# A gated linear-attention and two-layer MLP kernel: norm work spread between recurrence steps, wider VectorE operations, and weight decoding moved between VectorE and ScalarE

## The chip, the cores and the metric

The kernel runs on one core of a Trainium2 chip. A core has the engines PE (TensorE, matrix products), DVE (VectorE), ACT (ScalarE), POOL (GpSimd, which here only issues transfers) and SP (SyncE, transfers too). The metric is device time in microseconds of one launch; less is better. The kernel before took 1100.47 us, the median of three runs (1099.94 to 1103.4).

## The reference

The inputs are float32. First comes a complex, gated linear attention over batch 4, 8 heads, 768 positions and head size 48, then two MLP blocks over the 3072 tokens of width 384:

```python
mag = sqrt(a_re**2 + a_im**2)
scale = minimum(mag, 0.999) / (mag + 1e-6)
ar, ai = a_re * scale, a_im * scale            # per position t and row d
for t in range(768):
    S_re, S_im = ar[t]*S_re - ai[t]*S_im + outer(k[t], v[t]), ar[t]*S_im + ai[t]*S_re
    y[t] = q[t] @ S_re
x = y as 3072 x 384
x = ((x @ w1) * (x @ w2) @ w3) @ w_out         # w1, w2: 384 x 1024; w3: 1024 x 1024; w_out: 1024 x 384
h = x @ w_in                                   # 384 x 2048
out = (h * tanh(softplus(h))) @ w_out2         # 2048 x 384
```

The kernel's weights arrive as 64-bit floats in two 32-bit words each, the low and the top word.

## The kernel before, in words

**Attention by chunks.** The tokens are cut into 24 chunks of 128, eight to a group, three groups. For every chunk the running products of the gates are needed from the chunk's middle to both sides. `bh_stream(g)` (L178 on) makes them for the eight chunks of group g at once: 128 partitions hold chunk halves and heads, and the 65 positions of a half go in ten blocks of seven (`BLK`; the last has two). For each block it loads the gates into `an` and k and q into `kqt`, by transfers that POOL issues. `norm(i)` (L203 to L243) turns block i's gates into scaled gates (`an`, with one part in both signs) and a factor `rv`: ACT squares, takes an inverse root and makes polynomials, DVE multiplies and limits. `steps(i)` (L245 on) then runs the recurrence: per position two DVE products and a sum for the running product `p` (L261, L263) and a product for `rv` (L262). After a block's seven steps it multiplies k and q by the running products into `kt` (L273, one instruction for each of two halves) and POOL stores `kt` to memory, `kq_d`. After the group's last block a small table `mt` follows.

**Chunks.** `ch_stream` loads a chunk's scaled k and q from `kq_d` (`tm`), transposes them on PE (L372), ACT copies them to `kf` and `qf` (L373), PE forms the scores, DVE masks them into `am` (L416), PE makes the output (`ps_y`), which goes through memory (`xd`) into tiles of 512 tokens.

**Weights.** `decode` (L135 to L156) rebuilds float32 values from the two words: ACT's Abs of the scaled top word gives the value without its low three mantissa bits and sign; a 16-bit ACT copy (L151) brings the low word's upper half beside the top word's, one DVE instruction shifts and masks (L152), and another shifts the value and joins the bits (L155). It is used on 11 pieces of 1024 elements per partition in `fold_stream`, which multiplies w3 by w_out once on PE (`ps_f`, L171), and on 48 pieces of 384 elements: 16 for w1 and w2 (`w12`), 16 for w_in (`win_stream`), 16 for the last weight in the first token tile of the last stage. `split` (L130, L131) cuts float32 into two parts of reduced precision, and `mm3` makes three PE products of them.

**MLPs.** `m1_stream` runs the first block per tile of 512 tokens (`pa`, `pb`, `acc`), the last stage the second (`ps_h`, sigmoid L637, Ln L644, tanh L649, `ps_o`).

**Order.** `_merge` draws from several streams by the costs that they yield: first the fold with group 0's `bh_stream`; then chunks 0 to 7, group 1 and part of the first MLP; then chunks 8 to 15, group 2 and more of it; then the last chunks and the MLP with w_in's decode; then the rest. That order gives priorities. A planner in the framework takes, for each engine, the ready instruction of highest priority by its own estimate of time, so each engine's queue can differ from the source: in the trace, instructions of `norm` stand between those of `steps`. Tiles with `bufs=1` have one buffer, and a new writer waits for the last reader.

Of the kernel before, what the change touches and what calls it, by code (L numbers as in the profile page):

```python
# [64 lines left out]
def kernel(  # L65
# [30 lines left out]
    msk = const.tile([CMAX, sum(SIZES)], F32, name="msk")  # L96
    sg = const.tile([128, 1], F32, name="sg")
    n_blk = [-(-(l + 1) // BLK) for l in GROUPS]
    flags = const.tile([128, sum(n_blk) + 1], F32, name="flags")
    wsum = const.tile([128, 64], F32, name="wsum")  # L100
    cb = const.tile([128, 3], F32, name="cb")
    fss = [const.tile([64, 2, D], F32, name=f"fs{z}") for z in range(2)]
# [31 lines left out]

    def decode(src, n, dst=None, raw=None, pool=None, cap=False):  # L135

        if raw is None:
            raw = (pool or stg).tile([128, n, 2], I32, tag="raw64", name="raw64")
        nc.sync.dma_start(out=raw.rearrange("p n z -> p (n z)"), in_=src.bitcast(I32))
        t = dst if dst is not None else stg.tile([128, n], I32, tag="dec", name="dec")  # L140
        f = t.bitcast(F32)
        i = n_flags[0]
        if not cap:
            n_flags[0] += 1
        top, r16 = raw[:, :, 1], raw.bitcast(U16)
        A.activation(
            out=f, in_=top.bitcast(F32), func=AF.Abs, scale=W_SCALE, accum_out=None if cap else wsum[:, i:i + 1]
        )
        if cap:
            V.tensor_scalar(out=f, in0=f, scalar1=W_MAX, scalar2=None, op0=ALU.min)  # L150
        A.copy(out=r16[:, :, 2], in_=r16[:, :, 1])  # L151
        V.tensor_scalar(  # L152
            out=top, in0=top, scalar1=13, scalar2=-0x7FFFFFF9, op0=ALU.arith_shift_right, op1=ALU.bitwise_and
        )
        V.scalar_tensor_tensor(out=t, in0=t, scalar=3, in1=top, op0=ALU.logical_shift_left, op1=ALU.bitwise_or)  # L155
        return f  # L156

    def fold_stream():
# [7 lines left out]
        for j in range(8):  # L166
            raw, dst = bufs[j % 3]
            f = decode(w3t[:, j], 1024, dst, raw).rearrange("p (k m) -> p k m", k=8)
            ps = mm_p.tile([128, HD], F32, tag="mm", name="ps_f")
            for kk in range(8):  # L170
                T.matmul(ps, lhsT=f[:, kk], rhs=wos[:, kk], start=(kk == 0), stop=(kk == 7))  # L171
            split(ps, woh[:, j], wol[:, j])
            for z, w in enumerate((woh, wol)):
                nc.sync.dma_start(out=w3o_d[:, z, j], in_=w[:, j].bitcast(F32))
            yield 2.0
# [5 lines left out]
    def bh_stream(g):  # L181
# [3 lines left out]
        blocks = [(s0, min(s0 + BLK, L + 1)) for s0 in range(0, L + 1, BLK)]  # L185
        ans, kqs, dec = {}, {}, {}
        run = {}
# [9 lines left out]
        def load_kq(i):  # L197
# [3 lines left out]
            nc.gpsimd.dma_start(out=kqs[i].rearrange("p s z d -> p s (z d)"), in_=kq[:, k0 + s0:k0 + s0 + m])  # L201

        def norm(i):  # L203
            s0, s1 = blocks[i]
            n = s1 - s0
            an = ans.pop(i)
            pad = [128, BLK, D]
            sq = bh.tile([128, n, 2, D], F32, tag="sq", name="sq", bufs=1, padded_shape=[128, BLK, 2, D])
            A.activation(out=sq, in_=an[:, :, 1:3], func=AF.Square)
            m2 = bh.tile([128, n, D], F32, tag="m2", name="m2", bufs=1, padded_shape=pad)  # L210
            V.tensor_tensor(out=m2, in0=sq[:, :, 0], in1=sq[:, :, 1], op=add)
            yield .5
            y0 = bh.tile([128, n, D], F32, tag="y0", name="y0", bufs=1, padded_shape=pad)
            A.activation(out=y0, in_=m2, func=AF.Abs_reciprocal_sqrt)
            fl, y2 = sq[:, :, 0], sq[:, :, 1]
            A.activation(out=y2, in_=y0, func=AF.Square)
            V.tensor_tensor(out=y2, in0=m2, in1=y2, op=mul)
            yield .5
            A.activation(out=fl, in_=y0, func=AF.Square, bias=cb[:, 0:1])
            A.activation(out=fl, in_=fl, func=AF.Relu, bias=cb[:, 1:2], accum_out=flags[:, f0 + i:f0 + i + 1])  # L220
            V.scalar_tensor_tensor(out=y0, in0=y2, scalar=-3.0, in1=y0, op0=add, op1=mul)
            yield .5

            p1, p2 = sq[:, :, 0], sq[:, :, 1]
            A.activation(out=p1, in_=y0, func=AF.Identity, scale=0.5e-6, bias=1.0)
            A.activation(out=p2, in_=y0, func=AF.Identity, scale=-0.5e-6, bias=1.0)
            rv = bh.tile([128, n, D], F32, tag="rv", name="rv", padded_shape=pad)
            V.scalar_tensor_tensor(out=p1, in0=y0, scalar=-2.0 / 0.999, in1=p1, op0=ALU.max, op1=mul)
            yield .5
            V.scalar_tensor_tensor(out=an[:, :, 2], in0=an[:, :, 2], scalar=sg[:, 0:1], in1=p1, op0=mul, op1=mul)  # L230
            yield .5
            A.activation(out=an[:, :, 0], in_=an[:, :, 2], func=AF.Copy, scale=-1.0)  # L232
            V.scalar_tensor_tensor(out=an[:, :, 1], in0=an[:, :, 1], scalar=-0.4995, in1=p1, op0=mul, op1=mul)
            yield .5
            V.scalar_tensor_tensor(out=p2, in0=y0, scalar=-2.0 / 0.999, in1=p2, op0=ALU.min, op1=mul)
            yield .5
            A.activation(out=rv, in_=p2, func=AF.Square, scale=0.5)
            if i == 0:
# [3 lines left out]
                V.memset(rv[0:64, 0], 1.0)  # L242
            dec[i] = (an, rv)  # L243

        def steps(i):  # L245
            s0, s1 = blocks[i]
            n = s1 - s0
            an, rv = dec.pop(i)
            p = bh.tile([128, n, 2, D], F32, tag="p", name="p", padded_shape=[128, BLK, 2, D])
            for j in range(n):  # L250
# [14 lines left out]
            run["p"], run["rv"] = p[:, n - 1], rv[:, n - 1]  # L265
            m = min(s1, L) - s0
            if m > 0:
                kqt = kqs.pop(i)
                V.tensor_tensor(out=kqt[:, :, 1], in0=kqt[:, :, 1], in1=rv[:, 0:m], op=mul)
                yield .5  # L270
                kt = bh.tile([128, m, 2, 2, D], F32, tag="kt", name="kt", bufs=1, padded_shape=[128, BLK, 2, 2, D])
                for z in range(2):
                    V.tensor_tensor(out=kt[:, :, z], in0=_bc(kqt[:, :, z], 2, 2), in1=p[:, 0:m], op=mul)  # L273
                    yield .8
                nc.gpsimd.dma_start(out=kq_d[g][0:64, s0:s0 + m], in_=kt[0:64].rearrange("p s z r d -> p s (z r d)"))
                for z in range(2):
                    nc.gpsimd.dma_start(
                        out=kq_d[g][64:128, s0:s0 + m, (1 - z) * D2:(2 - z) * D2],
                        in_=kt[64:128, :, z].rearrange("p s r d -> p s (r d)"),
                    )  # L280
            if s0 <= L - 1 < s1:
# [4 lines left out]
                if g == 0:  # L286
                    nc.gpsimd.dma_start(out=fss[0][0:8], in_=last[120:128])
            if i < len(blocks) - 1:
                return
            fs = fss[g % 2]  # L290
            x1 = bh.tile([64, 2, 2, D], F32, tag="x1", name="x1", bufs=1)
            mt = bh.tile([64, 4, D], F32, tag="mt", name="mt", bufs=1)
            bt = p[0:64, L - s0]
            V.tensor_tensor(out=x1[:, 0], in0=bt, in1=fs, op=mul)
# [5 lines left out]
            tabs[g] = mt  # L300
            yield 1.0

        load(0)
        load(1)
        load_kq(0)
        yield from norm(0)
        for i in range(len(blocks)):
            if i + 2 < len(blocks):
                load(i + 2)
            if i + 1 < len(blocks):  # L310
                if blocks[i + 1][0] < L:
                    load_kq(i + 1)
                yield from norm(i + 1)
            yield from steps(i)

# [6 lines left out]
    def ch_stream():  # L322
# [41 lines left out]
        def tr(n):  # L364
            C = chunks[n][2]
            kf[n] = ch.tile([D2, H, C], F32, tag="kf", name="kf", bufs=1)
            qf[n] = ch.tile([D2, H, C], F32, tag="qf", name="qf")
            for z, dst in ((0, kf[n]), (1, qf[n])):
# [572 lines left out]
```

## Time and profile before

| | before |
|---|---|
| median of the runs | 1100.47 us |
| profiled execution | 1102.09 us, span 1100.3 us |
| PE busy | 936.0 us, 85% |
| DVE busy | 686.9 us, 62% |
| ACT busy | 680.6 us, 62% |
| POOL busy | 109.3 us, 10% |
| mean granted clock of TensorE | 0.941 of full speed |

The span is the profiled part of the execution; about 1.8 us lie around it. Busy shares are means over stages that differ. The stages are: up to about 160 us the fold and group 0; from there to about 415 us groups 1 and 2 with chunks and the first MLP; to about 690 us the remaining chunks and the first MLP; then the second MLP.

### The profile page before, as it was taken

The numbers are of one execution on the slowest core, as the hardware profiler recorded it, in microseconds if no ns is written. First come the engines' busy times: TensorE is split into PE (matmuls) and PEld (weight loads), VectorE is DVE, ScalarE is ACT, GpSimd is POOL, SyncE is SP. The second block draws the span as 40 slices with busy tenths as digits, with TensorE's granted clock in tenths as the row PEclk, the third lists the DMA queues.
The fourth block names the chain that finished last, engine by engine and source line by source line (L and its number), as shares of the span: only waits on it lengthen the run. The fifth ranks groups of instructions, "written<-read, shape, count | busy, mean of one in ns | idle before, by whom it ended". The sixth has DMA issues, their size and how long they took to land.

```text
span 1100.3 us, 14021 instructions
## 1 busy us (share of the span) xinstructions
PE 936.0 (85%) x4952; PEld 756.6 (69%) x4952; DVE 686.9 (62%) x1513; ACT 680.6 (62%) x1203; POOL 109.3 (10%) x161
## 2 busy tenths in 40 slices
PE   0584008799799789999989999999999999999997
PEld 0342007687587678888878878877888888888876
DVE  4789998998899975263233532688465545555452
ACT  6884467777866753383543642898666745566672
POOL 1122342221223211000000000000000000000000
PEclk9896559799999979999989999999999999999999
DMA  7785579975845985342562420240100101000000
GB/s 275 231 251 143 130 187 276 240 207 152 221 135 151 232 198 140 90 149 65 148 143 47 123 86 1 89 123 19 34 24 1 58 1 58 1 10 20 1 29 32
DMA packets 72511, 124.37 MB, mean 113 GB/s; under 512 B 7575, under 2 KB 45777, under 8 KB 71025
## 3 DMA queue, kind: packets, MB, share of 16 engines
q1 hardware_dynamic: 60880, 85.41, 28.0%
q0 software_dynamic: 11552, 37.98, 12.5%
q8 instruction: 41, 0.67, 0.3%
q14 instruction: 38, 0.30, 0.1%
HBM read 84.16 MB, written 36.18 MB: 109 GB/s over the span
## 4 chain that ended last, share of the span: by engine, by line
PE 59%; ACT 15%; DVE 11%; DMA 10%; issue 5%; POOL 0%; SPq 0%; DVEq 0%; ACTq 0%; POOLq 0%
PE ps_o L500 16%; PE ps_h L500 13%; PE pa L500 6%; PE pb L500 6%; PE acc L500 5%; DMA xl<-xd 3%; PE ps_f L171 3%; PE ps_tr L372 2%; DMA xd<-ysb 2%; PE ps_a L415 2%; ACT raw L151 2%; DVE t L261 2%; PE ps_y L433 2%; DVE kt L273 1%; DMA an<-in_a 1%
## 5 line engine op out<-in xcount | busy, mean ns | idle before, releaser
L500 PE MATMUL ps_o<-gh,wuh 128*128 128x512 f32 x288 | 112.5, 396 | 6.0 <-ACT gh L130 4.6
L500 PE MATMUL ps_o<-gl,wuh 128*128 128x512 f32 x288 | 113.1, 393 | 0.4 <-DVE gl L131 0.4
L500 PE MATMUL ps_h<-x2h,wil 128*128 128x512 f32 x288 | 113.2, 393 | 0.0
L500 PE MATMUL ps_h<-x2h,wih 128*128 128x512 f32 x288 | 113.2, 393 | 0.0
L500 PE MATMUL ps_o<-gh,wul 128*128 128x512 f32 x288 | 112.8, 392 | 0.0
L500 PE MATMUL ps_h<-x2l,wih 128*128 128x512 f32 x288 | 112.0, 389 | 0.0
L131 DVE TENSOR_TENSOR gl<-hb,gh 128x1024 fp32r<-128x1024 f32 x48 | 58.7, 1224 | 75.8 <-ACT gh L130 75.8
L637 ACT ACTIVATE wb<-ps_h 128x512 f32<-128x512 f32 x96 | 56.9, 604 | 71.6 <-PE ps_h L500 71.4
L638 DVE COPY hb<-ps_h 128x512 f32<-128x512 f32 x96 | 64.8, 688 | 47.6 <-ACT wb L637 45.5
L522 DVE TENSOR_TENSOR u<-u,pb 128x512 f32<-128x512 f32 x48 | 32.9, 685 | 89.4 <-PE pb L500 88.9
L372 PE MATMUL ps_tr<-id_sb,tm 128*96 128x128 f32 x384 | 58.7, 305 | 30.2 <-DMA tm<-kq_d 28.5
L372 PEld LDWEIGHTS ps_tr<-id_sb,tm 128*96 128x96 f32 x384 | 48.0, 141 | 39.3 <-issue 32.7
L500 PE MATMUL pa<-xh,w1h 128*128 128x512 f32 x144 | 60.2, 418 | 15.8 <-ACT xh L130 13.6
L130 ACT CAST gh<-hb 128x1024 fp32r<-128x1024 f32 x48 | 50.4, 1051 | 34.9 <-PE ps_o L500 34.9
L261 DVE TENSOR_TENSOR t<-an,p 128x192 f32<-128x192 f32 x192 | 67.9, 354 | 1.4 <-ACT an L232 1.3
L500 PEld LDWEIGHTS ps_o<-gh,wuh 128*128 128x128 f32 x288 | 53.6, 188 | 21.7 <-ACT gh L130 6.7
L519 ACT COPY u<-pa 128x512 f32<-128x512 f32 x48 | 28.3, 589 | 61.5 <-PE pa L500 61.4
L130 ACT CAST uh<-u 128x512 fp32r<-128x512 f32 x48 | 29.9, 623 | 58.8 <-DVE u L522 58.6
L500 PEld LDWEIGHTS ps_o<-gl,wuh 128*128 128x128 f32 x288 | 54.1, 188 | 12.5 <-DVE gl L131 0.8
L500 PEld LDWEIGHTS ps_h<-x2l,wih 128*128 128x128 f32 x288 | 54.1, 188 | 12.4
L500 PEld LDWEIGHTS ps_h<-x2h,wil 128*128 128x128 f32 x288 | 54.0, 188 | 12.5
L500 PEld LDWEIGHTS ps_o<-gh,wul 128*128 128x128 f32 x288 | 54.1, 188 | 12.0
(157 smaller groups left out, 2368.4 us busy)
## 6 DMA issues: line engine op xcount, KB each, us to landing
tm<-kq_d SPq DMA_DIRECT2D x48, 384.0 KB, 5.9
an<-in_a POOLq DMA_DIRECT2D x27, 336.0 KB, 5.1
kqt<-in_kq POOLq DMA_DIRECT2D x27, 336.0 KB, 5.1
kq_d<-kt POOLq DMA_DIRECT2D x54, 168.0 KB, 4.4
kq_d<-kt POOLq DMA_DIRECT2D x27, 336.0 KB, 4.2
vv<-in_v SPq DMA_DIRECT2D x24, 256.0 KB, 4.9
raw<-in_w SPq DMA_DIRECT2D x16, 384.0 KB, 4.7
raw<-in_win SPq DMA_DIRECT2D x16, 384.0 KB, 3.3
```

Source lines behind the costliest of these rows:

```text
L130: A.copy(out=hi, in_=raw)
L131: V.tensor_tensor(out=lo, in0=raw, in1=hi.bitcast(F32), op=sub)
L151: A.copy(out=r16[:, :, 2], in_=r16[:, :, 1])
L171: T.matmul(ps, lhsT=f[:, kk], rhs=wos[:, kk], start=(kk == 0), stop=(kk == 7))
L261: V.tensor_tensor(out=t, in0=win2, in1=_bc(pv[:, ::-1], 2, 2), op=mul)
L372: T.transpose(ps[:, hh], tm[n][:, h0 + hh, z], id_sb[0:C, 0:C])
L415: T.matmul(ps[:, hh], lhsT=kf[n][:, h], rhs=qf[n][:, h], start=True, stop=True)
L500: T.matmul(ps, lhsT=l, rhs=r, start=first and n == 0, stop=final and n == len(seq) - 1)
L519: A.copy(out=u, in_=pa)
L522: V.tensor_tensor(out=u, in0=u, in1=pb, op=mul)
L637: A.activation(out=wb[:, f % GRP], in_=ps, func=AF.Sigmoid, scale=-1.0)
L638: V.tensor_copy(hb[:, f % 2], ps)
```

## The change

`norm` does the same arithmetic in four turns (yields .5, 1.0, 1.3, .5) instead of eight pieces. Its first instruction, the squares, becomes a function of its own, issued a block earlier, ahead of the old block's `kt`. The other turns are drawn after steps 0, 2, 4 and 6 of the block before, no longer all ahead of that block's steps. Both parts of `an` are scaled by one DVE instruction; the factor -0.4995 moves into the polynomial, and both signs of one part are made by ACT with a scale per partition (`sg`). The two `kt` instructions become one. The group's state transfers come before `kt`, the table after everything.

`decode` takes the low word's top three bits with an ACT Relu (scale 2**-13, rounded on writing) into the whole low word, and DVE joins the top word's sign to it (and, or); DVE's shift and mask go. For fold tiles 2, 4 and 6 (`signs`) ACT makes the sign too: Relu into the lower half word, Sign in place on the top word, Identity into the upper half word; DVE then only joins. `qf` and `am` get one buffer instead of two.

```diff
-    def decode(src, n, dst=None, raw=None, pool=None, cap=False):
+    def decode(src, n, dst=None, raw=None, pool=None, cap=False, signs=False):
...
-        A.copy(out=r16[:, :, 2], in_=r16[:, :, 1])
-        V.tensor_scalar(
-            out=top, in0=top, scalar1=13, scalar2=-0x7FFFFFF9, op0=ALU.arith_shift_right, op1=ALU.bitwise_and
-        )
-        V.scalar_tensor_tensor(out=t, in0=t, scalar=3, in1=top, op0=ALU.logical_shift_left, op1=ALU.bitwise_or)
+        if signs:
+            r16 = raw.bitcast(U16)
+            A.activation(out=r16[:, :, 0], in_=r16[:, :, 1], func=AF.Relu, scale=2.0 ** -13, bias=cb[:, 3:4])
+            A.activation(out=top.bitcast(F32), in_=top.bitcast(F32), func=AF.Sign, bias=cb[:, 4:5])
+            A.activation(out=raw.bitcast(I16)[:, :, 1], in_=top.bitcast(F32), func=AF.Identity, scale=16384.0, bias=cb[:, 5:6])
+        else:
+            A.activation(out=low, in_=raw.bitcast(U16)[:, :, 1], func=AF.Relu, scale=2.0 ** -13, bias=cb[:, 3:4])
+            V.scalar_tensor_tensor(
+                out=low, in0=top, scalar=-0x80000000, in1=low, op0=ALU.bitwise_and, op1=ALU.bitwise_or
+            )
+        V.scalar_tensor_tensor(out=t, in0=t, scalar=3, in1=low, op0=ALU.logical_shift_left, op1=ALU.bitwise_or)
...
-            f = decode(w3t[:, j], 1024, dst, raw).rearrange("p (k m) -> p k m", k=8)
+            f = decode(w3t[:, j], 1024, dst, raw, signs=j in (2, 4, 6)).rearrange("p (k m) -> p k m", k=8)
...
+        def squares(i):
+            s0, s1 = blocks[i]
+            sqs[i] = bh.tile([128, s1 - s0, 2, D], F32, tag="sq", name="sq", bufs=1, padded_shape=[128, BLK, 2, D])
+            A.activation(out=sqs[i], in_=ans[i][:, :, 1:3], func=AF.Square)
...
+            yield .5
             V.tensor_tensor(out=y2, in0=m2, in1=y2, op=mul)
...
+            V.scalar_tensor_tensor(out=y0, in0=y2, scalar=-3.0, in1=y0, op0=add, op1=mul)
+
+            p1, p2 = m2, sq[:, :, 1]
+            A.activation(out=p1, in_=y0, func=AF.Identity, scale=-0.4995 * 0.5e-6, bias=cb[:, 6:7])
+            A.activation(out=p2, in_=y0, func=AF.Identity, scale=-0.5e-6, bias=1.0)
             A.activation(out=fl, in_=fl, func=AF.Relu, bias=cb[:, 1:2], accum_out=flags[:, f0 + i:f0 + i + 1])
...
+            yield 1.0
+            V.scalar_tensor_tensor(out=p1, in0=y0, scalar=-2.0 / 0.999, in1=p1, op0=ALU.max, op1=mul)
+            V.tensor_tensor(out=an[:, :, 1:3], in0=an[:, :, 1:3], in1=_bc(p1, 2, 2), op=mul)
+            A.activation(out=an[:, :, 0], in_=an[:, :, 2], func=AF.Copy, scale=sg[:, 0:1])
+            A.activation(out=an[:, :, 2], in_=an[:, :, 2], func=AF.Copy, scale=sg[:, 1:2])
+            yield 1.3
...
-            V.scalar_tensor_tensor(out=an[:, :, 2], in0=an[:, :, 2], scalar=sg[:, 0:1], in1=p1, op0=mul, op1=mul)
-            yield .5
-            A.activation(out=an[:, :, 0], in_=an[:, :, 2], func=AF.Copy, scale=-1.0)
-            V.scalar_tensor_tensor(out=an[:, :, 1], in0=an[:, :, 1], scalar=-0.4995, in1=p1, op0=mul, op1=mul)
...
-                for z in range(2):
-                    V.tensor_tensor(out=kt[:, :, z], in0=_bc(kqt[:, :, z], 2, 2), in1=p[:, 0:m], op=mul)
-                    yield .8
+                V.tensor_tensor(out=kt, in0=_bc(kqt, 3, 2), in1=_bc(p[:, 0:m], 2, 2), op=mul)
+                yield 1.6
...
-                yield from norm(i + 1)
-            yield from steps(i)
+            nxt = norm(i + 1) if i + 1 < NB else iter(())
+            run["r"] = dec[i][1]
+            for k, w in enumerate(steps(i)):
+                yield w
+                if k % 2 == 0:
+                    w = next(nxt, None)
+                    if w:
+                        yield w
+            yield from nxt
+            if i + 2 < NB:
+                squares(i + 2)
+            yield from scaled(i)
+        table()
+        yield 1.0
...
-            qf[n] = ch.tile([D2, H, C], F32, tag="qf", name="qf")
+            qf[n] = ch.tile([D2, H, C], F32, tag="qf", name="qf", bufs=1)
...
-            am = ch.tile([C, H, C], F32, tag="am", name="am")
+            am = ch.tile([C, H, C], F32, tag="am", name="am", bufs=1)
```

## Rows read from the trace of the kernel before

**Rows 1.** The page, busy totals and PE's slices of 27.5 us (tenths).
```profile
PE 936.0 (85%) x4952; PEld 756.6 (69%) x4952; DVE 686.9 (62%) x1513; ACT 680.6 (62%) x1203; POOL 109.3 (10%) x161
...
PE   0584008799799789999989999999999999999997
```

**Rows 2.** Busy time by stretch: start:end, length, busy us (instructions) by engine, clock, DMA.
```profile
9.50:46.40 36.90, 7.11 (x16) 3.78 (x16) 25.20 (x65) 36.13 (x55) 3.56 (x5) 0.98 0.74 255
46.40:97.20 50.80, 44.01 (x112) 24.54 (x112) 41.96 (x117) 34.49 (x54) 10.68 (x15) 0.85 0.74 216
97.20:160.50 63.30, 0.45 (x2) 0.25 (x2) 61.34 (x225) 34.03 (x80) 24.60 (x37) 0.52 0.58 153
...
160.50:289.50 129.00, 107.08 (x778) 90.53 (x779) 113.55 (x331) 95.98 (x231) 33.99 (x50) 0.91 0.83 224
289.50:415.00 125.50, 111.34 (x703) 93.38 (x702) 110.97 (x339) 86.34 (x208) 27.40 (x39) 0.94 0.71 179
610.00:640.00 30.00, 28.37 (x116) 22.72 (x117) 17.85 (x31) 23.32 (x44) 0.00 (x0) 0.94 0.52 157
690.00:760.00 70.00, 65.71 (x284) 52.59 (x283) 52.68 (x82) 68.39 (x105) 0.00 (x0) 1.00 0.27 80
...
415.00:1100.30 685.30, 666.04 (x3345) 544.09 (x3343) 332.56 (x432) 392.10 (x575) 4.76 (x8) 0.99 0.21 59
```

**Rows 3.** Chain of waits, 9.5 to 97 us: start, us, what.
```profile
13.47 2.44 ACT fw1l L151
...
46.42 8.10 PE ps_f L171 x16
...
83.83 13.34 PE ps_f L171 x32
```

**Rows 4.** DVE's groups by shape, the decode's lines: count, busy us, mean ns, idle before.
```profile
L155 DVE SCALAR_TENSOR_TENSOR dec<-dec,raw 128x384 int32<-128x384 int32 x48 | 26.3, 554 | 0.7
...
L152 DVE TENSOR_SCALAR raw<-raw 128x384 int32<-128x384 int32 x48 | 17.6, 370 | 23.4 <-ACT raw L151 23.0
...
L155 DVE SCALAR_TENSOR_TENSOR fw2h<-fw2h 128x1024 int32<-128x1024 int32 x3 | 3.7, 1223 | 0.0
...
L152 DVE TENSOR_SCALAR fw2h<-fw2h 128x1024 int32<-128x1024 int32 x4 | 2.8, 691 | 1.2 <-ACT fw2h L151 1.2
```

**Rows 5.** ACT's groups by shape.
```profile
L151 ACT COPY raw<-raw 128x384 uint16<-128x384 uint16 x48 | 51.4, 1076 | 0.3
...
L146 ACT ACTIVATE dec<-raw 128x384 f32<-128x384 f32 x48 | 27.3, 569 | 9.4 <-DMA raw<-in_w 6.3 <-DMA raw<-in_win 2.1 <-DMA raw<-in_wout 0.6
...
L219 ACT ACTIVATE sq<-y,cb 128x336 f32<-128x336 f32 x27 | 15.4, 570 | 0.0
...
L214 ACT ACTIVATE y<-m 128x336 f32<-128x336 f32 x27 | 13.5, 499 | 17.4 <-DVE m L211 17.4
...
L151 ACT COPY fw2h<-fw2h 128x1024 uint16<-128x1024 uint16 x4 | 10.3, 2570 | 0.1
...
L146 ACT ACTIVATE fw2h<-fw2h 128x1024 f32<-128x1024 f32 x3 | 3.6, 1186 | 0.0
```

**Rows 6.** Chain of waits, DVE's steps in a block (97 to 290 us).
```profile
104.58 0.48 DVE an L230
105.06 0.42 DVE an L233
...
122.21 1.54 DVE kt L273 x2
...
253.77 0.77 DVE kt L273
```

**Rows 7.** Chain of waits, a chunk's transposes.
```profile
173.90 1.81 PE ps_tr L372 x14
```

**Rows 8.** Waits of DVE, 100 to 165 us: us in total, times, longest.
```profile
DVE t L261 <- ACT an L232: 1.3, 1, 1.3
```

More of the change, by code (lines that the diff above doesn't have):

```diff
@@ L12 @@
 U16 = mybir.dt.uint16
+I16 = mybir.dt.int16
 I32 = mybir.dt.int32
@@ L96 @@
     msk = const.tile([CMAX, sum(SIZES)], F32, name="msk")
-    sg = const.tile([128, 1], F32, name="sg")
+    sg = const.tile([128, 2], F32, name="sg")
     n_blk = [-(-(l + 1) // BLK) for l in GROUPS]
@@ L100 @@
     wsum = const.tile([128, 64], F32, name="wsum")
-    cb = const.tile([128, 3], F32, name="cb")
+    cb = const.tile([128, 7], F32, name="cb")
     fss = [const.tile([64, 2, D], F32, name=f"fs{z}") for z in range(2)]
@@ L144, in decode @@
             n_flags[0] += 1
-        top, r16 = raw[:, :, 1], raw.bitcast(U16)
+        low, top = raw[:, :, 0], raw[:, :, 1]
         A.activation(
@@ L185, in bh_stream @@
         blocks = [(s0, min(s0 + BLK, L + 1)) for s0 in range(0, L + 1, BLK)]
-        ans, kqs, dec = {}, {}, {}
+        ans, kqs, dec, sqs = {}, {}, {}, {}
         run = {}
@@ L205, in norm @@
             n = s1 - s0
-            an = ans.pop(i)
+            an, sq = ans.pop(i), sqs.pop(i)
             pad = [128, BLK, D]
-            sq = bh.tile([128, n, 2, D], F32, tag="sq", name="sq", bufs=1, padded_shape=[128, BLK, 2, D])
-            A.activation(out=sq, in_=an[:, :, 1:3], func=AF.Square)
             m2 = bh.tile([128, n, D], F32, tag="m2", name="m2", bufs=1, padded_shape=pad)
             V.tensor_tensor(out=m2, in0=sq[:, :, 0], in1=sq[:, :, 1], op=add)
-            yield .5
             y0 = bh.tile([128, n, D], F32, tag="y0", name="y0", bufs=1, padded_shape=pad)
@@ L216, in norm @@
             A.activation(out=y2, in_=y0, func=AF.Square)
+            A.activation(out=fl, in_=y0, func=AF.Square, bias=cb[:, 0:1])
+            yield .5
             V.tensor_tensor(out=y2, in0=m2, in1=y2, op=mul)
-            yield .5
-            A.activation(out=fl, in_=y0, func=AF.Square, bias=cb[:, 0:1])
+            V.scalar_tensor_tensor(out=y0, in0=y2, scalar=-3.0, in1=y0, op0=add, op1=mul)
+            p1, p2 = m2, sq[:, :, 1]
+            A.activation(out=p1, in_=y0, func=AF.Identity, scale=-0.4995 * 0.5e-6, bias=cb[:, 6:7])
+            A.activation(out=p2, in_=y0, func=AF.Identity, scale=-0.5e-6, bias=1.0)
             A.activation(out=fl, in_=fl, func=AF.Relu, bias=cb[:, 1:2], accum_out=flags[:, f0 + i:f0 + i + 1])
[L221 to L226, printed above, removed]
-            rv = bh.tile([128, n, D], F32, tag="rv", name="rv", padded_shape=pad)
-            V.scalar_tensor_tensor(out=p1, in0=y0, scalar=-2.0 / 0.999, in1=p1, op0=ALU.max, op1=mul)
-            yield .5
-            V.scalar_tensor_tensor(out=an[:, :, 2], in0=an[:, :, 2], scalar=sg[:, 0:1], in1=p1, op0=mul, op1=mul)
-            yield .5
-            A.activation(out=an[:, :, 0], in_=an[:, :, 2], func=AF.Copy, scale=-1.0)
-            V.scalar_tensor_tensor(out=an[:, :, 1], in0=an[:, :, 1], scalar=-0.4995, in1=p1, op0=mul, op1=mul)
-            yield .5
+            yield 1.0
[4 more added lines that the diff above has]
+            yield 1.3
+            rv = bh.tile([128, n, D], F32, tag="rv", name="rv", padded_shape=pad)
             V.scalar_tensor_tensor(out=p2, in0=y0, scalar=-2.0 / 0.999, in1=p2, op0=ALU.min, op1=mul)
-            yield .5
             A.activation(out=rv, in_=p2, func=AF.Square, scale=0.5)
@@ L243, in norm @@
             dec[i] = (an, rv)
+            yield .5
         def steps(i):
@@ L248, in steps @@
             an, rv = dec.pop(i)
-            p = bh.tile([128, n, 2, D], F32, tag="p", name="p", padded_shape=[128, BLK, 2, D])
+            p = run["b"] = bh.tile([128, n, 2, D], F32, tag="p", name="p", padded_shape=[128, BLK, 2, D])
             for j in range(n):
@@ L265, in steps, with scaled @@
             run["p"], run["rv"] = p[:, n - 1], rv[:, n - 1]
+            if s0 <= L - 1 < s1:
+                last = p[:, L - 1 - s0]
+                nc.gpsimd.dma_start(out=fss[g % 2][8:64], in_=last[64:120])
+                nc.gpsimd.dma_start(out=fss[1 - g % 2][0:8], in_=last[120:128])
+                if g == 0:
+                    nc.gpsimd.dma_start(out=fss[0][0:8], in_=last[120:128])
+        def scaled(i):
+            s0, s1 = blocks[i]
             m = min(s1, L) - s0
             if m > 0:
-                kqt = kqs.pop(i)
-                V.tensor_tensor(out=kqt[:, :, 1], in0=kqt[:, :, 1], in1=rv[:, 0:m], op=mul)
+                kqt, p = kqs.pop(i), run["b"]
+                V.tensor_tensor(out=kqt[:, :, 1], in0=kqt[:, :, 1], in1=run["r"][:, 0:m], op=mul)
                 yield .5
                 kt = bh.tile([128, m, 2, 2, D], F32, tag="kt", name="kt", bufs=1, padded_shape=[128, BLK, 2, 2, D])
-                for z in range(2):
-                    V.tensor_tensor(out=kt[:, :, z], in0=_bc(kqt[:, :, z], 2, 2), in1=p[:, 0:m], op=mul)
-                    yield .8
+                V.tensor_tensor(out=kt, in0=_bc(kqt, 3, 2), in1=_bc(p[:, 0:m], 2, 2), op=mul)
+                yield 1.6
                 nc.gpsimd.dma_start(out=kq_d[g][0:64, s0:s0 + m], in_=kt[0:64].rearrange("p s z r d -> p s (z r d)"))
@@ L280, in steps, with table @@
                     )
-            if s0 <= L - 1 < s1:
-                last = p[:, L - 1 - s0]
-                nc.gpsimd.dma_start(out=fss[g % 2][8:64], in_=last[64:120])
-                nc.gpsimd.dma_start(out=fss[1 - g % 2][0:8], in_=last[120:128])
[L286 to L290, printed above, removed]
+        def table():
+            p, fs = run["b"], fss[g % 2]
             x1 = bh.tile([64, 2, 2, D], F32, tag="x1", name="x1", bufs=1)
             mt = bh.tile([64, 4, D], F32, tag="mt", name="mt", bufs=1)
-            bt = p[0:64, L - s0]
+            bt = p[0:64, L - blocks[-1][0]]
             V.tensor_tensor(out=x1[:, 0], in0=bt, in1=fs, op=mul)
@@ L300, in steps @@
             tabs[g] = mt
-            yield 1.0
+        NB = len(blocks)
         load(0)
@@ L305, in bh_stream @@
         load_kq(0)
+        squares(0)
         yield from norm(0)
-        for i in range(len(blocks)):
-            if i + 2 < len(blocks):
+        if NB > 1:
+            squares(1)
+        for i in range(NB):
+            if i + 2 < NB:
                 load(i + 2)
-            if i + 1 < len(blocks):
-                if blocks[i + 1][0] < L:
-                    load_kq(i + 1)
-                yield from norm(i + 1)
-            yield from steps(i)
+            if i + 1 < NB and blocks[i + 1][0] < L:
+                load_kq(i + 1)
+            nxt = norm(i + 1) if i + 1 < NB else iter(())
[7 more added lines that the diff above has]
+            yield from nxt
+            if i + 2 < NB:
+                squares(i + 2)
+            yield from scaled(i)
+        table()
+        yield 1.0
     x_t = {}
@@ L569 @@
     nc.sync.dma_start(out=msk, in_=mask)
-    V.memset(sg[0:64], 0.4995)
-    V.memset(sg[64:128], -0.4995)
-    tab = const.tile([128, 1], F32, name="tab")
+    for z in range(2):
+        V.memset(sg[0:64, z:z + 1], 1.0 - 2.0 * z)
+        V.memset(sg[64:128, z:z + 1], 2.0 * z - 1.0)
+    tab = const.tile([128, 2], F32, name="tab")
     A.activation(out=tab, in_=sg, func=AF.Abs_reciprocal_sqrt)
@@ L578 @@
     V.memset(cb[:, 2:3], -W_MAX)
+    V.memset(cb[:, 3:4], 2.0 ** -15 - 0.5)
+    V.memset(cb[:, 4:5], 2.0 ** -100)
+    V.memset(cb[:, 5:6], -16384.0)
+    V.memset(cb[:, 6:7], -0.4995)
     F = fold_stream()
```

## The prediction

> **What bounds the kernel now.** I read the busy totals first, then the busy time by stretch, then the chain of waits inside the stretches where no engine is full, then the groups by shape for prices.
>
> The totals say little: PE has 936 of 1100 us and its slices are full only from 412 us on [rows 1]. The stretches divide the run into five parts [rows 2]. From 9.5 to 46.4 us ACT is busy for 36.13 of 36.90 us, so this piece is as long as ACT's work. From 46.4 to 97.2 us PE has 44.0 of 50.8 us, with the fold of w3 and w_out; ACT has 34.5 and DVE 42.0. From 97.2 to 160.5 us DVE has 61.3 of 63.3 us and PE nothing: group 0's recurrence is finished by DVE alone. From 160.5 to 415 us PE has 86%, DVE 88% and ACT 72%, a mixture in which each waits for the others. From 415 us PE has 666 of 685 us, and what is missing there lies mostly at two places: 690 to 760 us, where ACT has 68.4 of 70 us and PE 65.7, and 610 to 640 us (PE 28.4 of 30). A microsecond saved counts therefore on ACT before 46 us, on DVE from 97 to 160 us, on both in part up to 415 us, and on ACT again around 630 and 700 to 760 us.
>
> The chain of waits shows what ACT does in the first stretch: the 16-bit copies of L151, 2.44 us each, are its largest piece, six of them by 46 us. From 46 us it changes to the fold's matmuls, 6.7 to 8.1 us a unit [rows 3].
>
> **The change part by part.** All prices are means of one instruction; where one instruction follows another closely on its engine, the chain's step is shorter than the duration, and I use the step.
>
> *Half words by ScalarE (no signs).* Per decode the 16-bit copy and VectorE's shift-and-mask go; a Relu from the 16-bit word to a 32-bit word and a two-tensor and/or come. On DVE that is 1.22 instead of 0.69 us for 1024 elements and 0.55 instead of 0.37 for 384 [rows 4]: +0.53 and +0.18. On ACT the Relu is not in the trace. Its lower end is the Abs, which reads the same words at the same spacing: 1.19 us for 1024 and 0.57 for 384, to which a bias read from memory adds 0.07 (570 against 499 ns at 336 elements). The upper end is the copy itself, 2.57 and 1.08 [rows 5]. The copy is the only 16-bit form on ACT and costs over twice the others; whether its reads or its 2-byte writes are slow, no row tells. The Relu writes whole words, so I take 1.26 and 0.64: 1.31 and 0.44 us saved per decode, with nothing saved as the other end.
>
> *Signs by ScalarE (fold tiles 2, 4, 6).* DVE loses one instruction (-0.69). ACT's copy becomes a Relu that again writes half words (2.57, or 1.26), and a Sign (1.26, by the Abs) and an Identity into the upper half word (1.26 to 2.57) are added: +2.5 us per tile in my sum, +1.2 to +3.8 at the ends.
>
> The Trainium skill, "ScalarE: Activation LUTs", section "What ACT_TABLE_LOAD costs", prices any ACTIVATE at 186 ns plus 0.833 ns per element and 93 ns per operand read from memory, the same for every function and for 16-bit data: an estimate of 1.13 us for each of these at 1024. The row of the copy (2.57 us) contradicts it for this kind of data; by the rule a signs tile would cost ACT only +0.8 us and the sum below would be 1.7 us lower by the signs tile of the first stretch. The same page's "Rules for kernel authors" puts multiplications and maxima on VectorE, which speaks against the signs: by the rows, ACT pays 2.5 us for 0.69 us of DVE. I count it so.
>
> *Norm.* Per full block DVE loses one of two scalings of `an` by p1: 0.48 + 0.42 become one two-row multiplication at 0.77 (a lone `kt` of the same 672 elements): -0.13. The two `kt` (1.54 together) become one of 1344; two single steps of 336 against 672 (0.42, 0.77) leave 0.07 of fixed cost, so 1.47: -0.07. Together -0.20 [rows 6]. On ACT a second sign copy comes with a scale from memory (0.57), and two others get such an operand (0.07 each): +0.72 us per block [rows 5]. The kernel has 27 full blocks: -5.4 us on DVE, +19 us on ACT.
>
> *Order.* Norm's pieces now stand between steps. The planner, not the source, sets each engine's order, and already DVE has only 2 us idle from 97 to 160 us: there is nothing to fill there. For the other stretches I take 0, with 8 us either way, about half of the 30 us that DVE lacks between 160 and 415 us.
>
> *Single buffers for qf and am.* The copy to qf must wait for the last products that read the old one, with ACT's later copies behind it. PE does those products before most of the new chunk's transposes, which take 1.81 us for 14 [rows 7], so cover is ample: 0; at worst some 0.4 us for 24 chunks. *Squares before `kt`* needs the load of `an`, issued a block earlier on POOL's queue; the two or three state transfers of a group's end now come ahead of the `kq_d` stores on that queue in the source: 0, at worst 1.5 us a group.
>
> **The sum**, against the profiled execution of 1102.09 us (span 1100.3):
> - 9.5 to 46.4 us, ACT one to one: five plain decodes -6.5, one signs tile +2.5, three blocks +2.2: -1.8.
> - 46.4 to 97.2 us: ACT -3.9, +5.0, +2.9 on 34.5 of 50.8 us; the fold's matmuls are the longer work: 0 (-4 to +4). The fold's extra DVE work in both stretches, 8 x 0.53 - 3 x 0.69 = +2.2 us, lies in DVE's 20.6 us of idle time.
> - 97.2 to 160.5 us: six blocks x -0.20: -1.2.
> - 160.5 to 289.5 us: w1 and w2 are decoded (16 decodes): ACT -7.0 and +6.7, DVE +2.9 and -1.9: about even, but the plain decode itself stands in the chain of its weights: -1.
> - 289.5 to 415 us: DVE -1.9, ACT +6.7 at 69% load: 0.
> - 610 to 640 us: up to eight decodes -0.44 each; PE lacks 1.6: -1.
> - 690 to 760 us: 16 decodes x 0.44 = 7.0 us less on the full engine, PE can win back the 4.3 it lacks: -4.
>
> That is -9.0: 1093.1 for an execution like the profiled one, which lay 1.6 us above the median of the runs; against the median 1100.47 it is 1091.5.
>
> **The rivals.**
> 1. *The order gives more than I count.* From 160 to 415 us DVE idles 30 us and PE 36; ACT's short operations no longer come in a bunch ahead of a block's steps. For it: no engine is full there. Against it: the planner already mixes norm and steps. The upper end of 8 us and the 4 us of the fold come on top: about 1080.
> 2. *The gain is hidden.* Group 0 ends by DVE's sum (128.5 us of work from 9.5 to 160.5 us by the three rows), so an earlier fold moves nothing, and 13 us more ACT work in groups 1 and 2 costs about 3 of the 5 won after 600 us: 1098.5, no change that can be told.
> 3. *Slower: half-word reads are what is slow.* Place: every Relu of a decode. Then it costs 2.57 and 1.08, nothing is saved, a signs tile adds 3.8. First stretch +3.8 + 2.2 = +6.0; second: ACT +10.5, on 34.5 of 50.8 us, +2; third -1.2; groups 1 and 2, where ACT gains 6.7 each and DVE 1.0 net: +2.5; after 600 us 0. +9.3: 1110. It decides from a Relu of about 2.0 us at 1024 elements up.
> 4. *Slower: the block's edge.* The scaling of `an` comes after step 4 of the old block. What covers ACT's two sign copies (1.2 us) is two steps, `kqt` and `kt`, some 3 us of DVE. If ACT's queue is over 2 us late there, the next block's first step waits, as it did once before (1.34 us) [rows 8]. At every second of 27 edges: +18 on the -9: 1109.5. ACT's 72% load speaks against so many.
>
> **How the numbers follow.** A difference under 0.3% (3.3 us) can't be told from no change in this kernel. Forecast 0.45 (own range 1085 to 1097), rival 1 0.18, rival 2 0.17, rival 3 0.12, rival 4 0.08. Faster: 0.45 x 0.97 + 0.18 + 0.03 = 0.65; slower: 0.12 + 0.08 - 0.01 = 0.19; the rest, 0.16, is the same. The range leaves out rival 3's middle and the far end of rival 1: 1076 to 1107.
>
> **What would show it.** Right: the Relu groups at 1.2 to 1.4 us (1024) and 0.6 to 0.7 (384); the first matmul of the fold some 2 us earlier; DVE's stretch before the first transposes still over 95% busy; PE over 69 of 70 us while w_out is decoded. Wrong: Relu over 2 us, or DVE's steps waiting for `an` at many block edges (rivals 3, 4); the start of the PE-filled part unmoved from 412 us (rival 2) or earlier by over 8 us (rival 1). The sum falls if the planner puts the decodes elsewhere, so that what ACT saves comes where it isn't full.

## The result, and the profile after

The changed kernel takes 1088.09 us (1085.56 to 1089.27, four runs) where the kernel before takes 1100.2 us beside it: the ratio is 0.9875, with a 95% interval of 0.9841 to 0.9909. A second set of runs gave 0.9874 (0.9846 to 0.9901). The profiled span went from 1100.3 to 1086.6 us, by 13.7 us.

The page's busy totals and PE's slices:

```profile
PE 934.8 (86%) x4952; PEld 756.3 (70%) x4952; DVE 690.5 (64%) x1456; ACT 681.7 (63%) x1239; POOL 109.0 (10%) x161
...
PE   0682029699699889999989999999999999999997
```

No engine has appreciably less to do than before [rows 1]: PE 1.2 us less, ACT 1.1 and DVE 3.6 us more. The time came out of waiting.

Busy time by stretch, columns as in [rows 2] (the rows from 160 us on are used further below):

```profile
9.50:46.40 36.90, 11.32 (x27) 6.28 (x28) 30.78 (x76) 35.98 (x62) 4.14 (x6) 1.00 0.82 277
46.40:90.50 44.10, 36.95 (x103) 20.43 (x101) 39.06 (x101) 35.96 (x56) 10.10 (x15) 0.92 0.77 233
90.50:154.30 63.80, 0.48 (x3) 0.23 (x2) 60.84 (x208) 40.57 (x94) 24.97 (x37) 0.53 0.64 158
...
160.00:420.00 260.00, 231.45 (x1550) 193.58 (x1549) 224.84 (x630) 186.85 (x453) 61.98 (x90) 0.91 0.77 199
420.00:676.00 256.00, 252.06 (x1535) 210.18 (x1534) 98.65 (x159) 112.72 (x252) 1.65 (x3) 0.99 0.36 96
610.00:640.00 30.00, 30.00 (x132) 24.37 (x132) 19.41 (x31) 19.23 (x39) 0.00 (x0) 1.00 0.45 152
676.00:748.00 72.00, 69.99 (x303) 56.28 (x302) 57.89 (x84) 66.09 (x109) 0.00 (x0) 1.00 0.29 88
```

In the same 36.9 us of a full ACT, DVE now gets 30.8 us of work done instead of 25.2 and PE has 27 of the fold's products behind it instead of 16 [rows 2]. The fold and group 0 end earlier. The fold's products, first the group with the first start and then the one with the last, before:

```profile
L171 PE MATMUL ps_f<-fw1h,fw1l x48: 486/486/1008, 34.7 to 91.5; 128*128 128x384 f32 x48
L171 PE MATMUL ps_f<-fw1h,fw2h x48: 486/486/1006, 46.4 to 96.7; 128*128 128x384 f32 x48
```

and after:

```profile
L178 PE MATMUL ps_f<-fw1h,fw1l x48: 486/486/1009, 35.0 to 82.7; 128*128 128x384 f32 x48
L178 PE MATMUL ps_f<-fw1h,fw2h x48: 486/486/590, 43.0 to 90.0; 128*128 128x384 f32 x48
```

Group 0's last `kt` starts at 144.7 us instead of 151.8. Busy time from 9.5 us to it, before and after:

```profile
9.50:151.80 142.30, 51.57 (x130) 28.57 (x130) 121.14 (x378) 99.62 (x176) 34.41 (x49) 0.76 0.67 202
9.50:144.70 135.20, 48.75 (x130) 26.95 (x130) 121.91 (x355) 105.33 (x193) 34.33 (x49) 0.79 0.72 213
```

DVE works 0.8 us more in it; its idle time fell from 21.2 to 13.3 us. PE needs 2.8 us less for as many products; the mean granted clock from 46.4 us is 0.85 to 97.2 us before [rows 2] and 0.92 to 90.5 us after. Whether that is a part of the gain or comes of it isn't shown.

From there on the three pieces of the run tell the rest: up to a chunk's first transposes, from there to the last stage's first product, and the last stage. The first starts stand in PE's lines for `ps_tr` and `ps_h` (durations min/median/max, then first and last start), before:

```profile
L372 PE MATMUL ps_tr<-id_sb,tm x384: 270/273/451, 163.7 to 601.2; 128*96 128x128 f32 x192
L500 PE MATMUL ps_h<-x2h,wih x288: 387/393/461, 687.4 to 1058.6; 128*128 128x512 f32 x144
```

and after:

```profile
L397 PE MATMUL ps_tr<-id_sb,tm x384: 270/273/449, 157.5 to 593.1; 128*96 128x128 f32 x192
L525 PE MATMUL ps_h<-x2h,wih x288: 387/393/504, 676.0 to 1044.7; 128*128 128x512 f32 x144
```

In these two profiles 6.2 us were won in the first piece, 5.3 in the second, 2.2 in the last.

ACT's groups, which show the prices that the prediction had to bound:

```profile
L158 ACT ACTIVATE raw<-raw,cb 128x384 int32<-128x384 uint16 x48 | 30.8, 642 | 9.5 <-DMA raw<-in_win 5.6 <-DVE u L547 2.2 <-DMA raw<-in_w 1.3
...
L239 ACT ACTIVATE an<-an,sg 128x336 f32<-128x336 f32 x27 | 15.5, 575 | 0.3
...
L158 ACT ACTIVATE fw1l<-fw1l,cb 128x1024 int32<-128x1024 uint16 x3 | 3.7, 1223 | 0.0
...
L154 ACT ACTIVATE fw2l<-fw2l,cb 128x1024 uint16<-128x1024 uint16 x1 | 2.6, 2599 | 0.0
L156 ACT ACTIVATE fw2l<-fw2l,cb 128x1024 int16<-128x1024 f32 x1 | 2.6, 2597 | 0.0
...
L155 ACT ACTIVATE fw2l<-fw2l,cb 128x1024 f32<-128x1024 f32 x1 | 1.2, 1220 | 0.0
```

A Relu that reads half words and writes whole ones takes 1223 ns; the same Relu that writes half words takes 2599, and so does an Identity that reads whole words and writes half ones. What is slow is the spaced 2-byte write, whatever is read; a 2-byte write of ACT without gaps isn't in these kernels.

And DVE's changed groups:

```profile
L290 DVE TENSOR_TENSOR kt<-kqt,p 128x1344 f32<-128x1344 f32 x27 | 41.9, 1551 | 0.3 <-DMA kq_d<-kt 0.3
...
L159 DVE SCALAR_TENSOR_TENSOR raw<-raw 128x384 int32<-128x384 int32 x48 | 26.4, 555 | 14.0 <-ACT raw L158 14.0
...
L237 DVE TENSOR_TENSOR an<-an,m 128x672 f32<-128x672 f32 x27 | 22.9, 849 | 0.0
```

### The profile page after: what moved, and what is told of

Read it like the earlier page. It is cut to its first block, busy times and chain, and to the rows that moved or that the text cites. A ratio compares the mean times of both kernels' runs of the same rounds, so it can differ in the third digit from the quotient of the medians.

```text
span 1086.6 us, 13948 instructions
## 1 busy us (share of the span) xinstructions
PE 934.8 (86%) x4952; PEld 756.3 (70%) x4952; DVE 690.5 (64%) x1456; ACT 681.7 (63%) x1239; POOL 109.0 (10%) x161
## 4 chain that ended last, share of the span: by engine, by line
PE 56%; DMA 4%; ACT 4%; DVE 3%; issue 1%; SPq 0%; DVEq 0%; ACTq 0%
PE ps_o L525 16%; PE ps_h L525 15%; PE pa L525 6%; PE acc L525 6%; PE pb L525 6%; PE ps_a L440 2%; PE ps_tr L397 2%; PE ps_y L453 1%; PE ps_u L405 1%; DMA ws<-w 1%; PE ps_y L458 1%; DMA xd<-ysb 1%; DMA raw<-in_wout 1%; DMA xl<-xd 1%; DMA vv<-in_v 0%
## 5 line engine op out<-in xcount | busy, mean ns | idle before, releaser
L397 PEld LDWEIGHTS ps_tr<-id_sb,tm 128*96 128x96 f32 x384 | 45.8, 138 | 34.8 <-issue 27.4
L525 PE MATMUL acc<-uh,woh 128*128 128x512 f32 x144 | 57.8, 407 | 8.5 <-ACT uh L131 8.5
L525 PEld LDWEIGHTS ps_h<-x2h,wih 128*128 128x128 f32 x288 | 54.0, 188 | 12.5 <-DVE hb L668 1.1
L525 PEld LDWEIGHTS ps_h<-x2l,wih 128*128 128x128 f32 x288 | 54.1, 188 | 12.4
```

Of the source, the lines that this page charges most:

```text
L397: T.transpose(ps[:, hh], tm[n][:, h0 + hh, z], id_sb[0:C, 0:C])
L525: T.matmul(ps, lhsT=l, rhs=r, start=first and n == 0, stop=final and n == len(seq) - 1)
```

## The experiments

The ratio is always to the kernel before on the same chip, in runs side by side. The three pieces are read from each kernel's profile as above (the first piece of after ends at 157.45 us). A profile is one execution: that of late decode back lay 4.9 us above the median of its kernel's runs, that of new norm alone 3.3 above, that of after at rate 104 3.6 below, so a few us in one second piece mean little.

| kernel | ratio (95%) | first piece | second | last |
|---|---|---|---|---|
| before | 1 | 163.7 | 523.8 | 412.8 |
| after | 0.9875 (0.9841 to 0.9909) | 157.4 | 518.5 | 410.6 |
| after again | 0.9874 (0.9846 to 0.9901) | 157.2 | 518.9 | 410.7 |
| new decode alone | 0.9928 (0.9907 to 0.9949) | 159.4 | 523.2 | 410.8 |
| new norm alone | 1.0023 (0.9998 to 1.0048) | 161.1 | 533.2 | 413.1 |
| no signs | 0.9909 (0.9888 to 0.9930) | 163.4 | 516.4 | 410.9 |
| order back | 0.9938 (0.9916 to 0.9960) | 157.8 | 525.9 | 412.1 |
| signs in six tiles | 0.9929 (0.9902 to 0.9956) | 164.6 | 517.8 | 412.3 |
| narrow operations | 0.9920 (0.9889 to 0.9951) | 154.4 | 526.5 | 411.6 |
| late decode back | 0.9908 (0.9873 to 0.9943) | 158.3 | 527.7 | 412.8 |
| after, rate 104 | 0.9951 (0.9932 to 0.9971) | 156.9 | 522.9 | 410.7 |
| after, rate 108 | 0.9722 (0.9690 to 0.9753) | 157.5 | 502.2 | 410.6 |
| before, rate 104 | 1.0009 (0.9982 to 1.0036) | 158.0 | 530.3 | 413.2 |
| before, rate 108 | 1.0074 (1.0048 to 1.0101) | 161.5 | 537.6 | 413.2 |

**The changed kernel once more**, unchanged, beside others on its chip, to see how far a ratio moves between two sets of runs: by 0.0001.

> The changed kernel once more, as the yardstick for the runs beside it: 1086 to 1090 us, ratio 0.986 to 0.990; group 0's table at 136 to 137 us.

**Which half of the change: decode alone, norm alone.**

```diff
 # decode alone: the kernel before, with decode(), signs=j in (2, 4, 6) and cb's constants of after
 # norm alone: the kernel after, with
-    def decode(src, n, dst=None, raw=None, pool=None, cap=False, signs=False):
+    def decode(src, n, dst=None, raw=None, pool=None, cap=False):   # as before
```

> The kernel before with the new decode (Relu into whole words, signs by ScalarE in fold tiles 2, 4 and 6) and nothing else of the change. Theory D (the decode's saved ScalarE time is the gain: in the first 46 us, where ScalarE is full, and after 600 us): group 0's last kt starts 5 to 7 us earlier than the 151.8 us of before, the last 500 us gain some 6 us, 1088 to 1091 us in all. Rival N (the gain before 160 us comes from norm's new order and operations): group 0 ends within 2 us of before, only the late part is won, 1094 to 1096 us.

> The kernel after with the decode of before (16-bit copy, shift and mask, no signs): norm, steps, kt, squares, single buffers as changed. Theory D: ScalarE has 0.72 us more per block and saves nothing, so 1099 to 1104 us, group 0 not earlier than before. Rival N: group 0's last kt some 5 us earlier, 1093 to 1096 us.

The decode alone gives 0.7%, the norm nothing or a loss: theory D as to the cause. The sizes aren't theory D's: group 0's last `kt` starts 4.4 us earlier (147.4 us), not 5 to 7, and 1094.8 us is the time that rival N gave, where theory D had 1088 to 1091. The two together give 1.25%, more than their sum; the rate runs below say how far that excess can be trusted.

**The signs: none, three tiles, six.**

```diff
-            f = decode(w3t[:, j], 1024, dst, raw, signs=j in (2, 4, 6)).rearrange("p (k m) -> p k m", k=8)
+            f = decode(w3t[:, j], 1024, dst, raw).rearrange("p (k m) -> p k m", k=8)              # no signs
+            f = decode(w3t[:, j], 1024, dst, raw, signs=j >= 2).rearrange("p (k m) -> p k m", k=8) # six
```

> The kernel after with signs off: all 11 fold pieces take the plain decode (ScalarE 3 x 5.1 us less work at 1.22 instead of 2.6 + 1.2 + 2.6, VectorE 3 x 1.22 more). Theory D, by ScalarE's work: three tiles x 5.1 us come off ScalarE while it is full or nearly so, group 0 ends 2 to 5 us earlier, 1084 to 1087 us. Rival V (VectorE's sum holds group 0, so what goes to VectorE costs): group 0 ends up to 3.7 us later, 1089 to 1091 us.

> The kernel after with signs by ScalarE in six fold tiles (2 to 7) instead of three: VectorE 3 x 1.22 us less, ScalarE 3 x 5.1 us more between 46 and 95 us. Theory V (VectorE's sum holds group 0 and ScalarE has room there, 36 of 44 us busy): the three tiles gave about 5 us at group 0's table, three more give another 2 to 4: table at 133 to 135 us, 1084 to 1087 us. Rival A (ScalarE is full with three): 15 us more on an engine with 8 us of room makes the fold and group 0 later by 4 to 8 us: table at 140 to 144, 1092 to 1096 us.

Without signs ACT's busy time falls by 12.6 us, from 681.7 to 669.1, and the first piece is 6.0 us longer. That refutes theory D's reading. Rival V had the direction and gave up to 3.7 us. No engine is full from 46.4 to 90.5 us, but up to group 0's last `kt`, now at 150.0 us, DVE's work counts:

```profile
46.40:90.50 44.10, 32.14 (x88) 17.44 (x87) 36.80 (x85) 25.80 (x49) 9.73 (x14) 0.92 0.71 211
9.50:150.00 140.50, 48.36 (x130) 26.56 (x130) 125.30 (x357) 93.22 (x189) 34.29 (x49) 0.79 0.69 205
```

DVE has 3.4 us more to do than after's 121.91, the three and/or of 1.22 us each, and idles 15.2 us instead of 13.3. So 3.4 of the 5.3 us by which that `kt` is later are rival V's, and 1.9 are waiting.

ACT's waits from 9.5 to 95 us without signs show what is late next:

```profile
ACT fw2h L158 <- DMA fw2h<-in_w3t: 5.1, 1, 5.1
ACT fw1l L158 <- DMA fw1l<-in_w3t: 5.1, 2, 3.9
ACT fw2l L147 <- DMA fw2l<-in_w3t: 2.2, 1, 2.2
```

and with signs in three tiles, over the same stretch:

```profile
ACT fw1l L154 <- DMA fw1l<-in_w3t: 0.3, 1, 0.3
```

With less to do per piece, ACT's queue reaches the next piece of w3 before its load has landed (12.4 us in four waits instead of 0.3 in one), and norm's instructions stand behind it. That this is what DVE's 1.9 us come from wasn't tried by itself. With six tiles ACT is full:

```profile
46.40:90.50 44.10, 32.76 (x83) 17.50 (x82) 33.58 (x93) 44.10 (x58) 9.94 (x15) 0.88 0.74 223
9.50:152.30 142.80, 52.13 (x130) 27.88 (x130) 120.92 (x354) 120.16 (x205) 34.29 (x49) 0.79 0.69 204
```

and the first piece is 7.2 us longer, as rival A said: up to group 0's last `kt`, now at 152.3 us, DVE has 1.0 us less to do than with three and idles 21.9 us instead of 13.3. At this rate three tiles lie between two limits; none and six were not run at another.

**Order, wide operations.**

```diff
 # order back: norm whole, ahead of the steps
-            for k, w in enumerate(steps(i)):
...
             yield from nxt
+            yield from steps(i)
 # narrow operations
-            V.tensor_tensor(out=an[:, :, 1:3], in0=an[:, :, 1:3], in1=_bc(p1, 2, 2), op=mul)
-            A.activation(out=an[:, :, 0], in_=an[:, :, 2], func=AF.Copy, scale=sg[:, 0:1])
-            A.activation(out=an[:, :, 2], in_=an[:, :, 2], func=AF.Copy, scale=sg[:, 1:2])
+            V.scalar_tensor_tensor(out=an[:, :, 2], in0=an[:, :, 2], scalar=sg[:, 1:2], in1=p1, op0=mul, op1=mul)
+            A.activation(out=an[:, :, 0], in_=an[:, :, 2], func=AF.Copy, scale=-1.0)
+            V.tensor_tensor(out=an[:, :, 1], in0=an[:, :, 1], in1=p1, op=mul)
...
-                V.tensor_tensor(out=kt, in0=_bc(kqt, 3, 2), in1=_bc(p[:, 0:m], 2, 2), op=mul)
+                for z in range(2):
+                    V.tensor_tensor(out=kt[:, :, z], in0=_bc(kqt[:, :, z], 2, 2), in1=p[:, 0:m], op=mul)
```

> The kernel after, but norm of the next block is again drawn whole, ahead of the block's steps (all operations as after, squares still issued ahead of kt). Theory D: the planner mixes them anyway, 1087 to 1090 us. Rival N: the four turns are what shortened the first 160 us, 1092 to 1096 us and group 0 ends 4 us or more later.

> The kernel after with the narrower VectorE operations of before: two scalings of an and one sign copy by ScalarE, two kt. VectorE +0.20 us per block, ScalarE -0.6 per block. Theory V: group 0's table 1.5 to 2.5 us later, groups 1 and 2 about even, 1089 to 1092 us. Rival A (ScalarE's extra 0.6 us per block costs as much as the wide operations win): the same time as after, 1086 to 1089 us.

The order does nothing in the first piece (157.8 against 157.4 us), so rival N's reason falls, though 1095.4 us is the time that it gave: 7.4 us are lost in the second. The narrow operations are 3.0 us faster in the first piece and 8 us slower in the second. Neither fits a theory that goes by an engine's sum, and the larger differences lie in the second piece, where the queues of PE, DVE and ACT are woven by the planner.

**The late decodes.**

```diff
-                decode(win[:, f], 3 * 128), ...
+                decode_b(win[:, f], 3 * 128), ...                                  # decode of before
-                split(decode(wout[:, f], HD), wuh[:, f], wul[:, f])
+                split(decode_b(wout[:, f], HD), wuh[:, f], wul[:, f])
```

> The kernel after with the decode of before for w_in and the last weight (32 pieces of 384). Prediction's terms for these: about 1 us before the last stage and 4 in it. Theory D: the first output products come after the last stage's start by 31 us as after, but PE has 66 instead of 68 of the 70 us in which the last weight is decoded, and it lacks 1.6 us where w_in is: 1091 to 1093 us. Rival H (other work hides it): 1088 to 1089 us.

The first 72 us of the last stage, in this kernel:

```profile
686.00:758.00 72.00, 67.73 (x293) 54.19 (x291) 52.13 (x81) 68.57 (x107) 0.00 (x0) 1.00 0.29 88
```

with the new norm and the old decode:

```profile
694.30:766.30 72.00, 67.73 (x291) 54.04 (x290) 51.91 (x81) 68.32 (x106) 0.00 (x0) 1.00 0.29 88
```

and with the new decode and the old norm:

```profile
682.50:754.50 72.00, 69.88 (x301) 55.87 (x301) 57.63 (x83) 65.63 (x109) 0.00 (x0) 1.00 0.29 88
```

In the first 72 us of the last stage PE gets 67.7 to 67.8 us in all five kernels with the old decode there and 69.9 to 70.2 in all nine with the new one, whatever the rest: theory D, and the cleanest effect of the change, 2.2 us. What PE waited for in these 72 us, before and after:

```profile
PE ps_o L500 <- ACT gh L130: 4.3, 4, 1.6
```

```profile
PE ps_o L525 <- ACT gh L131: 0.8, 1, 0.8
PE ps_h L525 <- DVE hb L668: 0.6, 1, 0.6
PE ps_o L525 <- DVE gl L132: 0.6, 2, 0.4
```

The time with the old decode, 1095.7 us beside 1089.6 for the changed kernel, lies above theory D's 1091 to 1093; in its profile it is the second piece that is longer, too.

**How much is the planner's.** The streams' rate is the only thing changed; it moves priorities by 2%.

```diff
-    _merge((F, 44.0), (bh_stream(0), 106.0))
+    _merge((F, 44.0), (bh_stream(0), 108.0))     # and in the other two merges; 104.0 alike
```

> The kernel after with the group streams' rate 104 instead of 106 in the three merges: the same instructions, priorities moved by 2 per cent. Theory P (order and wide operations, each worth nothing beside the new decode alone but 0.5 per cent together, are largely the planner's fall of the queues): the time moves by 3 us or more against after's 0.9874, most likely up, to 0.990 to 0.994. Rival S (they are sound in themselves): within 0.2 per cent of 0.9874.

> The kernel after with rate 108: as rate 104 the other way. Theory P: 0.990 to 0.995. Rival S: 0.9855 to 0.9895.

> The kernel before with rate 104. Theory P: the kernel before falls as widely, 0.996 to 1.006 of itself, and off 1.000 by 0.3 per cent or more. Rival S: 0.998 to 1.002.

> The kernel before with rate 108. Theory P: 0.996 to 1.006 of itself, off 1.000 by 0.3 per cent or more. Rival S: 0.998 to 1.002.

The same instructions take 0.9722 to 0.9951 of before's time after the change, and 1.0000 to 1.0074 before it. Theory P holds for the changed kernel, which moves by 8 us or more both ways (0.9951 and 0.9722 against 0.9875); the kernel before stays within rival S's bounds at 104 and leaves both at 108. Rate 108 fell far better after the change than either expected: 1070.18 us, 2.8% under the kernel before and the best version here. Busy time of that kernel from 160 us to the last stage:

```profile
160.00:420.00 260.00, 240.00 (x1613) 200.38 (x1611) 229.00 (x639) 190.85 (x465) 61.90 (x90) 0.93 0.77 199
...
420.00:659.70 239.70, 239.53 (x1472) 200.00 (x1472) 92.57 (x148) 108.33 (x240) 1.65 (x3) 1.00 0.39 102
```

PE idles 20.2 us in it, where the changed kernel at rate 106 idles 32.5 (28.55 and 3.94, by the rows of its profile above). Its first and last pieces are those of after (157.5 and 410.6 us). At each of the three rates the changed kernel is the faster one, by 1.25% at 106, 0.6% at 104 (0.9951 / 1.0009) and 3.5% at 108 (0.9722 / 1.0074), and its second piece is the shorter, by 5, 7 and 35 us. At the three rates tried the sign is therefore the change's; its size at one rate isn't. That holds for the first piece too: before it takes 158.0 to 163.7 us by the rate alone, after 156.9 to 157.5, so the 6.2 us won at 106 are 1.1 at 104 and 4.0 at 108. Only the last piece gains alike, 2.2 to 2.6 us.

## Why the prediction was right

The time (1091.5 forecast, 1088.1 measured) and the sign were right, and so were the Relu's price and the last stage, by which the prediction reasoned. All three pieces came out at another size, and the term for the signs with the wrong sign. That the sum came so close is in part luck: it gave 3.2 and 3.3 us too little gain in two pieces and 1.8 too much in the third, and the same change is worth 0.6% at rate 104 and 3.5% at 108.

*The Relu.* 1.26 and 0.64 us were taken, 1.22 and 0.64 measured. Rival 3 needed 2.0. The Trainium skill's rule of one cost for every kind of data (1.13 us estimated, "ScalarE: Activation LUTs", section "What ACT_TABLE_LOAD costs") is good to 0.1 us for whole-word writes and short by 1.47 us for half-word ones, where the row was to be believed.

*The first 160 us: -3.0 forecast, -6.2 measured.* The sum had a start of the fold's matmuls 2 us earlier as its sign, and that failed: 35.0 us instead of 34.7. ACT is as full as before to 46 us, but more comes out of it, as the five cheap Relus promised. The term that was mis-sized is that of 46.4 to 97.2 us, put at 0 because the fold's matmuls are the longer work: the last of them start 6.7 us earlier, and DVE idles 7.9 us less up to group 0's last `kt`. The kernel before wins 5.7 us of the first piece by its rate alone, so not all of this is the decode's. The term for the signs failed. Its price on ACT was the upper end, 2.60 + 1.22 + 2.60 against 2.57: +3.85 us per tile. But I booked it as a loss, and taking the signs away costs 6.0 us here. I had left the fold's extra work on DVE to DVE's idle time, where 3.4 us of it showed up in full, and I had not looked at what ACT's queue would meet when it got ahead, the load of the next piece.

*Norm's operations: -1.2 forecast in this piece.* The two instructions are as priced: 1551 and 849 ns long, and the next instruction starts 1.47 and 0.77 us after them (`kt` at 101.88 us, the scaling at 106.19 us). Of the six blocks counted here only three are full blocks of group 0; one is its short last one and two are group 1's. DVE stays at 95% of its stretch, and the narrow forms are 3.0 us faster in the first piece. Whether ACT's extra copies or the longer `kt` cost that isn't settled.

*160 us to the last stage: -2 forecast, -5.3 measured.* Of it 1.6 us is the place of w_in's decode, where PE now has 30.0 of 30 us instead of 28.4 [rows 2]: -1 was forecast. PE's last gap before its full part ends at 395.8 us instead of 398.1, between the signs of rivals 1 and 2. The rest can't be told from the planner's fall: I gave the order 0, with 8 us either way, and rival 1 the upper end of that. The rates show that 8 us was too narrow for it: 502 to 523 us after the change, 524 to 538 before. The separate ratios, 0.992 to 0.994 for the decode alone, the order back and the narrow operations, lie within the spread of the changed kernel (0.972 to 0.995) and can't be read as prices of the parts.

*The last stage: -4 forecast, -2.2 measured.* PE wins back 2.3 of the 4.3 us that it lacked; ACT has 66.1 of 72 us, no longer full. The sign, PE over 69 of 70 us, failed: what PE still lacks, 2.0 us of 72, is a wait for ACT's `gh` only in 0.8 us; the others are for DVE, which has 57.9 us there instead of 52.1 in a kernel with the old decode.

*Rival 4 and the single buffers.* Waits of DVE at a block's edge:

```profile
DVE rv L269 <- ACT rv L243: 2.6, 2, 1.8
DVE t L268 <- ACT an L239: 1.9, 3, 1.2
```

Five waits and 4.5 us in the whole run, instead of one of 1.3 [rows 8]: there, but not at every second of 27 edges. ACT's copy to `qf` waits as before only for its transposes:

```profile
ACT qf L398 <- PE ps_tr L397: 6.4, 7, 1.7
```

## What to carry to other kernels

Before moving work onto an engine, look at what the new instruction writes: the same function cost 1.22 or 2.60 us by the width of its spaced writes alone. An engine with idle time isn't free: count its work and its idle time up to the point that others wait for, as with DVE's three and/or, which cost 3.4 us of the 5.3 there. And where a planner weaves the queues, run both kernels at one or two neighbouring priorities before crediting a part of a change: here 2% on a rate moved the time by up to 1.5%, more than the whole change.

## What was not expected of the hardware

ACT's spaced 2-byte writes run at 2.60 us for 1024 elements against 1.22 for 4-byte writes at the same spacing, from 16-bit and from 32-bit sources alike.
